# GpSimd's scatters of the last four groups, in rows or one and two at a time

## The chip, the core and the metric

The kernel runs on one core of one Trainium2 chip. Its time is device microseconds of one execution of the whole program. The core has five engines with a queue each: TensorE (PE in the profile; its weight loads are PEld), VectorE (DVE), ScalarE (ACT), GpSimd (POOL) and SyncE (SP, which here only starts DMAs). A queue with a q behind its name, POOLq or SPq, is the sequencer of that engine. Semaphores order what the engines do, and an instruction that waits holds back everything behind it on its own engine. The DMAs that SP starts run as "hardware" queue q1, those that GpSimd starts as "software" queue q0.

## The reference

A linear attention with decay, of 4 batches, 8 heads, 768 steps and 48 channels, is followed by a mixture of experts in which each of the 3072 tokens goes to the one expert with the largest logit.

```python
# attention, per batch and head; state is 48 x 48
cur   = (u * k_t) outer v_t
y_t   = r_t @ (state + cur)
state = w * state + k_t outer v_t

# experts: x is y, 3072 rows of 384 (all heads); 8 experts of width 1024
logits = x @ w_gate + modality_bias[modality_id]
e      = argmax(logits);  gate = softmax(logits)[e]
out    = gate * (relu(x @ w1[e]) @ w2[e])
```

The rows of `x` therefore have to be gathered by expert before the two expert products, and the result has to go back to the row of its token.

## The kernel before

**Units and groups.** The attention is cut into 24 units (`NU`): 6 chunks of 128 steps times 4 batches, chunk by chunk. A unit gives 128 tokens of 384 features. The routing works on groups of units, `GROUPS = ((0, 4), (4, 8), (8, 12), (12, 16), (16, 19), (19, 22), (22, 24))`. I call them group 0 to group 6; the last four are units 12 to 15 (four units), 16 to 18 (three), 19 to 21 (three) and 22 to 23 (two).

**What becomes of a group.** `token` adds the two parts of a unit's output and squares it on ScalarE (L431); `high` (ScalarE, L454) and `low` (VectorE, L458) write it as two 16-bit halves into the group's `row` tile, of which there are three in turn; `flip` transposes it by a DMA of SP; `logits` is on TensorE; `choose`, `count` and `place` find the expert and, in `posi`, the row of each token in a DRAM table `rows` that is sorted by expert. `sign` writes the token's number into the row (GpSimd). Then `send` (L570) scatters one unit, 128 rows of 1544 bytes, into `rows` with an indirect DMA whose descriptors GpSimd makes. There are 24 such sends.

**When a send is issued.** All engines are in an order written out by hand (`manual_schedule`), so the order of the Python calls is the order in each queue. In the loop over units (L1090 on) the units up to 20 issue one or two sends apart from each other, with GpSimd's elementwise work (`decay` L311, `carry` L318, `own_keys` L323) between them. From unit 21 on (`late`) this is left out and the sends come in rows: group 3's four sends at the end of unit 21, group 4's three in the tail after the last unit's `token`, and group 5's three and group 6's two directly behind each other in the tail. With `spaced=True` each is preceded by a memset of one element (`gap`, L569).

**Experts that start early.** While the attention still runs, nine blocks of 128 rows of the first expert (`s_` functions, slots 0 to 8) are computed between the units: `s_turn` has SP transpose the rows from `rows` into one of two halves of `mxT` (L893), `s_up` is 36 matmuls with f16 weights in two parts (L906), `s_high` and `s_low` make the halves of the hidden layer (L910, L915), `s_down` is 24 matmuls (L980, L985), `s_take` scales on ScalarE, and `s_give` sends the result to the output with an indirect DMA of GpSimd (L876), which I call an output send.

**The tail.** After the loop (L1168 on) the last unit and slots 5 to 8 are interleaved with the routing of groups 4, 5 and 6. `setup3` writes constants on GpSimd, `ends` and `pads` have SP write nine blocks of empty rows behind the experts' rows (L803), `jobs` makes the table of the remaining blocks on VectorE. The first block after that, `turn(0, self.s_row(NE), m2, group="first")`, waits for all rows of the table that it may read; `up("a")` on it begins the steady loop over the remaining blocks (L1320 on), whose time the order of the sends does not touch.

**Who waits for a send.** The code declares the sends independent of each other ("rows") and of the `s_turn`s ("read", rows that were there before). It does not declare them independent of the first block after the slots ("first"). The `row` tile of group 6 is that of group 3, so the first write of group 6 (`token` of unit 22, ScalarE L431) waits until group 3's sends have read theirs.

Of the kernel before, what the change touches and what calls it, by code (L numbers as in the profile page):

```python
# [13 lines left out]
I16 = mybir.dt.int16  # L14
# [4 lines left out]
P = 128  # L19
B, H, S, D = 4, 8, 768, 48  # L20
# [3 lines left out]
DM = H * D  # L24
# [23 lines left out]
ROW, CODE, MORE = range(3)  # L48
SP, ACT, AD = (mybir.EngineType.SP,), (mybir.EngineType.Activation,), (mybir.EngineType.Activation, mybir.EngineType.DVE, mybir.EngineType.Pool)
WQ = 2 * WC // NQ  # L50

LOW, TOP = 64 - D, 64 + D
HALVES = slice(0, 64), slice(64, TOP)
# [2 lines left out]
class _Kernel:  # L56
# [121 lines left out]
    def setup2(self):  # L178

        nc, c = self.nc, self.c  # L180
        wg, bias, mod = self.raw_in
        self.gap = c.tile([1, 1], F32, name="gap")
        self.ctl = c.tile([1, 64], I32, name="ctl")
        wq = c.tile([P, DC * E], F32, name="wgsq")
        ssq = c.tile([P, 1], F32, name="wgssq")
        nc.scalar.activation(wq, wg, AF.Square, accum_out=ssq)
        yield
        self.tri = c.tile([P, P], F16, name="tri")
        nc.scalar.copy(self.tri, self.mask)
        yield  # L190
        pt = self.ps_r.tile([P, 512], F32, tag="r", name="pswg")
        nc.tensor.matmul(pt[:, :1], self.ones, ssq, start=True, stop=True)
        s = c.tile([P, 1], F32, name="wgs")
        self.wginv = c.tile([P, 1], F32, name="wginv")
        yield from self.pow2_(pt[:, :1], s, self.wginv, WGC, "wg")
        self.wghl = c.tile([P, DC, 2, E], F16, name="wghl")
        wg3 = wg.rearrange("p (d e) -> p d e", d=DC)
        nc.scalar.activation(self.wghl[:, :, 0, :], wg3, AF.Copy, scale=s)
        yield
        nc.vector.scalar_tensor_tensor(self.wghl[:, :, 1, :], wg3, s, self.wghl[:, :, 0, :], ALU.mult, ALU.subtract)  # L200
        yield
        NTT = NT // P
        mf = c.tile([P, NTT], F32, name="modf")
        nc.scalar.copy(mf, mod.rearrange("p (t w) -> p t w", w=2)[:, :, 0])
        yield
        mg = c.tile([P, NTT], F32, name="modg")
        nc.scalar.activation(mg, mf, AF.Copy, scale=-1.0, bias=1.0)
        yield
        self.lb = c.tile([P, NTT, E], F32, name="lb")
        lb2 = c.tile([P, NTT, E], F32, name="lb2")  # L210
        bc = lambda ap: ap.unsqueeze(1).to_broadcast([P, NTT, E])
        tb = lambda ap: ap.unsqueeze(2).to_broadcast([P, NTT, E])
        nc.vector.tensor_mul(self.lb, tb(mf), bc(bias[:, E:]))
        yield
        nc.vector.tensor_mul(lb2, tb(mg), bc(bias[:, :E]))
        yield
        nc.vector.tensor_add(self.lb, self.lb, lb2)
        yield
# [338 lines left out]
    def sign(self, u):  # L557
        n, lo = u["n"], u["lo"]
        row = u["row"][:, :n, 2 * DM + 2 :].bitcast(I32).rearrange("p b o -> p (b o)")
        self.nc.gpsimd.tensor_copy(row, self.tok[:, lo : lo + n])  # L560

    def send(self, u, k, spaced=False):

# [252 lines left out]
    def norm(self, junk, q):  # L816
        self.nc.scalar.activation(junk, self.raw[:, q * WQ : (q + 1) * WQ], AF.Square, accum_out=self.ssq[:, q : q + 1])

# [21 lines left out]
    def piece(self, q, part, parts, n=1):  # L840
        w = WQ // parts
        return slice(q * WQ + part * w, q * WQ + part * w + n * w), self.ws[:, 2 * q // NQ : 2 * q // NQ + 1]

# [149 lines left out]
    def run(self):  # L993
# [20 lines left out]
        self.slot = {}  # L1014
        junk = m.tile([P, WQ], F16, name="junk", bufs=1)
        groups = {}
# [15 lines left out]
        def chain(*gs):  # L1032
            for g in gs:
                yield from g
# [37 lines left out]
        def route(i, d, f, *args):  # L1072
            for lo, hi in GROUPS:
                if hi - 1 + d == i and lo in groups:
                    f(groups[lo], *args)

        def each(i, *fs):
            for f in fs:
                if live(i):
                    f(i)  # L1080
# [9 lines left out]
        for i in range(NU - 1):  # L1090
            each(i + 5, self.turned)
            each(i + 4, self.lines)
            each(i + 1, self.scores, self.own_keys)
            route(i, 3, lambda u: fills.append(self.choose(u)))
            route(i, 5, lambda u: fills.append(chain(self.place(u), self.ahead(ahead[u["lo"]], u)) if u["lo"] in ahead else self.place(u)))
            up, down = ups.get(i), ups.get(i - 1)
            if up is not None:
                self.s_up(up, 0)
            if down is not None:
                self.s_high(down, 1)  # L1100
                self.s_down(down, 0)
            self.token(i - 1) if i else None
            if ups.get(i - 2) is not None:
                self.s_take(ups[i - 2])
            if i and i - 1 == self.grp["lo"]:
                groups[i - 1] = self.grp
            fill()
            each(i, self.taken) if i else None
            for j in range(2):
                each(i - 1, lambda i: self.state(i, j))  # L1110
                fill()
            if down is not None:
                self.s_low(down, 1)
                self.s_due(down)
            begin.get(i, lambda: None)()
            late = i >= NU - 3
            for k in range(2):
                if not late:
                    for d in (6, 7):
                        route(i, d, self.send, 1)  # L1120
                if k == 0:
                    each(i + 3, self.decay)
            if ups.get(i - 2) is not None:
                self.s_give(ups[i - 2])
            each(i + 2, self.carry)
            route(i, 4, self.sign)
            each(i + 2, self.keys)
            if i:
                fac = self.factor(i - 1)
                for _ in fac:  # L1130
                    fill()
            self.own(i, 0)
            each(i - 1, self.high)
            for j in range(2):
                each(i + 1, lambda i: self.causal(i, j))
                fill()
            self.own(i, 1)
            each(i - 1, self.low)
            if up is not None:
                self.s_high(up, 0)  # L1140
                self.s_low(up, 0)
            fill()
            each(i - 1, self.flip)
            fill()
            self.values(i)
            if up is not None:
                self.s_up(up, 1)
            if down is not None:
                self.s_down(down, 1)
            for p in range(2):  # L1150
                for h in range(2):
                    c, r = divmod(i + 1 - 2 * p - h, B)
                    if r == 0 and 0 < c < NCH - 1:
                        self.fade(c, slice(2 * p, 2 * p + 2), range(2 * h, 2 * h + 2))
            if any(hi - 1 + d == i for lo, hi in GROUPS for d in (4, 5)):
                fill(99)
            route(i, 2, self.logits)
            route(i, 4, self.count)
            if late:
                for d in (5, 6, 7):  # L1160
                    route(i, d, self.send, B, True)
            for f in at.get(i, ()):
                f()
            for k in turns.get(i, ()):
                self.s_turn(k)


        g4, g5 = (groups.get(lo) for lo, _ in GROUPS[-3:-1])  # L1168
        run = lambda g, n: [next(g, None) for _ in range(n)]
        i, j = NU - 2, NU - 1  # L1170
# [5 lines left out]
        self.own(j, 1)  # L1176
        p4 = chain(self.place(g4), self.ahead(ahead[g4["lo"]], g4))
        run(p4, 99)
        self.s_take(4)
        fac = self.factor(i)  # L1180
        run(fac, 9)
# [5 lines left out]
        self.values(j)  # L1187
        self.s_up(5, 1)
        self.token(j)
        self.send(g4, B, True)  # L1190
        self.s_give(4)
        g6 = groups.setdefault(GROUPS[-1][0], self.grp)
        self.setup3()
# [5 lines left out]
        run(fac, 9)  # L1199
        self.s_high(5, 1)  # L1200
        self.high(j)
        self.s_low(5, 1)
        self.low(j)
        self.logits(g5)
# [19 lines left out]
        self.s_low(6, 1)  # L1224
        run(c6, 9)
        run(p5, 99)
        self.send(g5, B, True)
        self.s_down(6, 0)
        self.count(g6)
        self.s_down(6, 1)  # L1230
        run(p6, 99)
        self.send(g6, B, True)
        self.s_take(6)
        self.s_up(7, 0)
        self.s_high(7, 0)
# [56 lines left out]
        def second_half(code):  # L1292
            with tc.If(code % 8 > 3) as first:
# [6 lines left out]
                nc.gpsimd.tensor_tensor(self.whi[:, hi], self.raw[:, hi], sc.to_broadcast([P, 512]), ALU.mult)  # L1300
                mid = slice(sl.start - WQ, hi.start)
                nc.scalar.activation(self.whi[:, mid], self.raw[:, mid], AF.Copy, scale=sc)
# [75 lines left out]
```

## Time and profile before

| | |
|---|---|
| median of 3 runs | 377.9 us (375.51 to 379.3) |
| profiled execution | 379.97 us |
| its span, first to last instruction | 378.0 us |
| busy: PE, DVE, ACT, POOL | 345.8, 226.0, 178.3, 164.1 us |
| mean granted TensorE clock | 0.952 of full |
| sends to `rows` | 24, mean 1001 ns on GpSimd |
| `rk` products on GpSimd | 24, mean 1274 ns |

A line of the timeline gives start and duration in us, the engine, the line of the kernel, the operation, the tiles (written <- read), the shape, how many instructions were merged, and in brackets how long the engine had been idle before and what ended that. "issue" means that the engine waited for nothing that the profile shows. A line of the view by windows gives, for a stretch, the busy time of each engine with its count of instructions in brackets, then the granted TensorE clock, the busy share of the DMA engines, and GB/s. The view of waits gives total, number and longest wait in us.

### The profile page before, as it was taken

The numbers are of one execution on the slowest core, as the hardware profiler recorded it, in microseconds if no ns is written. First come the engines' busy times: TensorE is split into PE (matmuls) and PEld (weight loads), VectorE is DVE, ScalarE is ACT, GpSimd is POOL, SyncE is SP. The second block draws the span as 40 slices with busy tenths as digits, with TensorE's granted clock in tenths as the row PEclk, the third lists the DMA queues.
The fourth block names the chain that finished last, engine by engine and source line by source line (L and its number), as shares of the span: only waits on it lengthen the run. The fifth ranks groups of instructions, "written<-read, shape, count | busy, mean of one in ns | idle before, by whom it ended". The sixth has DMA issues, their size and how long they took to land. (4 is left out here: it accounts for less than half of the span.)

```text
span 378.0 us, 14983 instructions
## 1 busy us (share of the span) xinstructions
PE 345.8 (91%) x5387; PEld 271.7 (72%) x5387; DVE 226.0 (60%) x762; ACT 178.3 (47%) x479; POOL 164.1 (43%) x231
## 2 busy tenths in 40 slices
PE   8799999697999999969899699998999999999883
PEld 3577777566978878758787477886677778877661
DVE  7668999889897875844447342338633323224861
ACT  7467875696756756554431112228022222256811
POOL 7996867736637855170424311123421111202631
PEclk9999999959699999987989899999999999999998
DMA  6999999999938998560333532111862122111110
GB/s 170 267 178 185 225 199 249 301 243 211 224 58 223 240 280 188 84 197 4 109 61 107 209 87 64 42 42 42 316 91 57 42 46 59 42 42 42 42 54 4
DMA packets 60749, 50.29 MB, mean 133 GB/s; under 512 B 46872, under 2 KB 54311, under 8 KB 60448
## 3 DMA queue, kind: packets, MB, share of 16 engines
q1 hardware_dynamic: 57504, 40.21, 48.1%
q0 software_dynamic: 3200, 9.47, 7.2%
q8 instruction: 30, 0.49, 0.5%
q14 instruction: 15, 0.12, 0.1%
HBM read 28.39 MB, written 11.83 MB: 106 GB/s over the span
## 5 line engine op out<-in xcount | busy, mean ns | idle before, releaser
L906 PEld LDWEIGHTS <-whi 128*128 128x128 f16 x1248 | 76.5, 101 | 8.7 <-issue 5.7
L980 PEld LDWEIGHTS <-hh 128*128 128x128 f16 x416 | 38.2, 98 | 31.2 <-ACT hh L910 6.3
L906 PE MATMUL phb<-mxT,whi 128*128 128x128 f16 x768 | 50.9, 219 | 0.0
L352 ACT ACTIVATE dv<-kv,d 128x48 f32<-128x48 f32 x192 | 47.9, 323 | 3.5 <-DVE d L344 3.3
L323 POOL TENSOR_TENSOR rk<-rc,kc 128x512 f32<-128x512 f32 x24 | 30.6, 1274 | 39.9 <-DVE posi L552 13.8
L906 PEld LDWEIGHTS <-wlo 128*128 128x128 f16 x624 | 39.8, 101 | 3.2 <-DVE wlo L852 3.2
L910 ACT ACTIVATE hh<-phb 128x256 f16<-128x256 f32 (+1 forms) x48 | 21.4, 454 | 42.3 <-PE po L980 18.0
L915 DVE SCALAR_TENSOR_TENSOR hl<-phb,hh 128x256 f16<-128x256 f32 (+1 forms) x48 | 24.2, 511 | 24.8 <-ACT hh L910 14.5
L906 PE MATMUL phs<-mxT,whi 128*128 128x128 f16 x432 | 32.7, 237 | 3.8 <-issue 3.8
L311 POOL TENSOR_TENSOR rc<-ud,powr 128x512 f32<-128x512 f32 (+1 forms) x27 | 32.8, 1219 | 3.2 <-PE py L394 1.5
L401 PE MATMUL py<-kv,at 128*64 128x48 f32 x768 | 30.0, 229 | 4.6 <-issue 4.6
L570 POOL DMA_INDIRECT rows<-row,posi x24 | 24.0, 1001 | 22.8 <-issue 17.1
L372 DVE TENSOR_TENSOR at<-psc,mask 128x512 f32<-128x512 f32 x48 | 31.6, 682 | 3.6 <-PE psc L366 3.3
L906 PE MATMUL phb<-mxT,wlo 128*128 128x128 f16 x384 | 30.0, 219 | 2.5 <-DVE wlo L852 2.5
L401 PEld LDWEIGHTS py<-kv,at 128*64 128x64 f32 x768 | 27.7, 146 | 6.0 <-issue 5.7
L990 DVE TENSOR_SCALAR fac<-mt,wf 128x1 f32<-128x1 f32 x17 | 3.6, 212 | 44.7 <-ACT otb L866 39.0
L985 PEld LDWEIGHTS <-hl 128*128 128x128 f16 x208 | 19.2, 97 | 14.8 <-issue 3.3
L980 PE MATMUL po<-wlo,hh 128*128 128x384 f16 x136 | 28.0, 326 | 1.7 <-DVE wlo L852 1.7
L980 PE MATMUL po<-whi,hh 128*128 128x384 f16 x136 | 28.6, 327 | 0.9 <-ACT hh L910 0.9
L866 ACT ACTIVATE otb<-po,fac 128x384 f32<-128x384 f32 x16 | 9.2, 578 | 42.1 <-PE phb L906 37.1
L366 PE MATMUL psc<-rc,kc 48*64 48x128 f32 (+1 forms) x768 | 28.3, 286 | 0.8 <-issue 0.8
L366 PEld LDWEIGHTS psc<-rc,kc 48*64 48x64 f32 (+1 forms) x768 | 22.1, 139 | 9.1 <-issue 4.1
(251 smaller groups left out, 641.7 us busy)
## 6 DMA issues: line engine op xcount, KB each, us to landing
ud<-in_pd SPq DMA_DIRECT2D x24, 384.0 KB
kv<-in_pt SPq DMA_DIRECT2D x24, 384.0 KB
raw<-in_w SPq DMA_DIRECT2D x12, 512.0 KB
raw<-in_w SPq DMA_DIRECT2D x2, 1536.0 KB, 6.4
rows<-pad SPq DMA_DIRECT2D x10, 193.0 KB
rows<-row,posi POOLq DMA_INDIRECT x24
xT<-row SPq DMA_TRANSPOSE x23
xn<-rows SPq DMA_TRANSPOSE x17
```

The source lines that it names most:

```text
L311: nc.gpsimd.tensor_mul(u["rc"][:, s], u["rT"][:, s], self.powr[:, s])
L323: nc.gpsimd.tensor_mul(u["rk"], u["rc"], u["kc"])
L352: nc.scalar.activation(u["dv"][:, sl], u["v"][:, sl], AF.Copy, scale=u["d"][:, h : h + 1])
L366: nc.tensor.matmul(u["ps"][j][s, pr * P : (pr + 1) * P], u["kc"][r, pr, s], u["rc"][r, pr, :], start=True, stop=True)
L372: nc.vector.tensor_mul(u["at"][:, j * NPR : (j + 1) * NPR, :], u["ps"][j].rearrange("p (q t) -> p q t", q=NPR), self.mask.unsqueeze(1).to_ ...
L401: nc.tensor.matmul(py[t, sl], u["at"][:, j * NPR + pr, t], u["v"][:, sl], start=c == h == 0, stop=h == H - 1, skip_group_check=True)
L570: i = nc.gpsimd.indirect_dma_start(out=self.rows, out_offset=bass.IndirectOffsetOnAxis(ap=u["posi"][:, b : b + 1], axis=0), in_=u["row"][: ...
L906: self.nc.tensor.matmul(ph[:, q * P : (q + 1) * P], w[:, c0 : c0 + P], self.xT[:, xq, t * P : (t + 1) * P], start=i == q == 0, stop=i == l ...
L910: self.nc.scalar.activation(self.hh[:, f0 : f0 + fb, t * P : (t + 1) * P], p3, AF.Relu)
L915: self.nc.vector.scalar_tensor_tensor(self.hl[:, f0 : f0 + fb, r], p3, 0.0, self.hh[:, f0 : f0 + fb, r], ALU.max, ALU.subtract)
L980: self.nc.tensor.matmul(po[:, :DM], self.hh[:, f, t * P : (t + 1) * P], w[:, c0 : c0 + DM], start=n == q == f == 0, stop=False)
L985: self.nc.tensor.matmul(po[:, :DM], self.hl[:, f, t * P : (t + 1) * P], self.whi[:, c0 : c0 + DM], start=False, stop=f == FB - 1)
```

## The change

The rows of sends are taken apart. In units 21 and 22 group 3's four sends are issued two to a unit: one where the earlier units have them, and one after the second half of `own` on ScalarE. What holds the latter back is the new function `rest`, which on GpSimd copies one element of a tile that another engine has just written into `gap`, so that GpSimd waits for that engine, or, without an argument, clears a tile of 128 x 1536 16-bit numbers (`pause`). In the tail group 4's sends are issued one by one: after `place`, after the last unit's square, and after the last unit's `high`. Group 5 sends two, then there is a `pause`, then its third and group 6's first, another `pause`, and group 6's second. The number of sends and what each writes stay as they are.

```diff
+PAUSE = 1536
...
+        self.pause = c.tile([P, PAUSE], I16, name="pause")
...
+    def rest(self, of=None):
+
+        v = self.nc.gpsimd
+        if of is None:
+            v.memset(self.pause, 0)
+        else:
+            v.tensor_copy(self.gap, of)
...
             late = i >= NU - 3
-            for k in range(2):
-                if not late:
-                    for d in (6, 7):
-                        route(i, d, self.send, 1)
+            for k in range(1 if late else 2):
+                for d in (6, 7):
+                    route(i, d, self.send, 1)
                 if k == 0:
                     each(i + 3, self.decay)
...
             self.own(i, 1)
+            if late:
+                for d in (6, 7):
+                    route(i, d, lambda u: (self.rest(self.ctx_[i]["dv"][:1, DM - 1 :]), self.send(u, 1)))
             each(i - 1, self.low)
...
             route(i, 4, self.count)
-            if late:
-                for d in (5, 6, 7):
-                    route(i, d, self.send, B, True)
...
         run(p4, 99)
+        self.send(g4, 1, True)
         self.s_take(4)
...
         self.token(j)
-        self.send(g4, B, True)
+        self.rest(self.grp["ssq"][:1, self.ctx_[j]["at_g"] :][:, :1])
+        self.send(g4, 1)
         self.s_give(4)
...
         self.high(j)
+        self.rest(self.ctx_[j]["x16"][:1, :1])
+        self.send(g4, 1)
         self.s_low(5, 1)
...
         run(p5, 99)
-        self.send(g5, B, True)
+        self.send(g5, 2, True)
         self.s_down(6, 0)
         self.count(g6)
         self.s_down(6, 1)
         run(p6, 99)
-        self.send(g6, B, True)
+        self.rest()
+        self.send(g5, 1)
+        self.send(g6, 1, True)
+        self.rest()
+        self.send(g6, 1)
         self.s_take(6)
```

## The prediction

> **What bounds the kernel now.** I began with the page.
>
> ```profile
> span 378.0 us, 14983 instructions
> PE 345.8 (91%) x5387; PEld 271.7 (72%) x5387; DVE 226.0 (60%) x762; ACT 178.3 (47%) x479; POOL 164.1 (43%) x231
> ```
>
> TensorE is busy for 91% of the span and GpSimd for 43%. The chain that ended last covers only the last few microseconds, so I went on to TensorE's waits, over the span.
>
> ```profile
> PE py L401 <- issue: 4.6, 8, 1.1
> ...
> PE phs L906 <- issue: 3.8, 7, 1.2
> ...
> PE psc L366 <- issue: 0.8, 1, 0.8
> ...
> PE pst L339 <- issue: 0.7, 2, 0.5
> PE pst L408 <- issue: 0.5, 2, 0.3
> ```
>
> These are waits for nothing that the profile shows: 8.4 us in the first two rows, 2.0 us in the others. The timelines of TensorE and GpSimd place the 8.4 us: all of it beside the three rows of sends. The view by windows round the rows:
>
> ```profile
> 163.00:170.00 7.00, 3.58 (x60) 2.99 (x59) 1.80 (x6) 2.42 (x7) 5.85 (x12) 0.81 0.64 185
> ...
> 184.00:189.00 5.00, 3.62 (x62) 3.04 (x60) 2.24 (x10) 1.07 (x2) 3.91 (x8) 0.88 0.36 128
> ...
> 207.00:213.00 6.00, 2.48 (x24) 1.51 (x22) 0.22 (x1) 0.45 (x1) 3.76 (x8) 0.89 0.64 234
> ```
>
> The first count in brackets is TensorE's matmuls, and the third number from the right its granted clock. While GpSimd sends, TensorE gets through few matmuls and its clock is cut. No other engine is full there: VectorE and ScalarE wait for TensorE. So these stretches bound the time, and a row is paid twice, as standstill and as a slow clock.
>
> **What a row costs.** I time TensorE's steps in the disturbed units against the same steps undisturbed.
>
> ```profile
> 157.08 1.09 PE L401 MATMUL py<-kv,at 128*64 128x48 f32 x32
> 158.00 0.60 PE L339 MATMUL pst<-uw,rk 112*64 112x2 f32 x16
> ...
> 161.40 1.51 PE L906 MATMUL phs<-mxT,whi 128*128 128x128 f16 x24
> ...
> 163.51 0.88 PE L394 MATMUL py<-st,rc 112*64 112x96 f32 x16
> 164.23 0.50 PE L401 MATMUL py<-kv,at 128*64 128x48 f32 x10
> ...
> 170.94 2.74 PE L906 MATMUL phs<-mxT,whi 128*128 128x128 f16 x24
> ...
> 174.58 1.10 PE L366 MATMUL psc<-rc,kc 64*64 64x128 f32 x32
> ...
> 184.78 0.74 PE L401 MATMUL py<-kv,at 128*64 128x48 f32 x20
> ...
> 191.52 0.60 PE L481 MATMUL pr<-wghl,xT 128*128 128x16 f16 x18
> ...
> 207.17 0.33 PE L906 MATMUL phs<-mxT,whi 128*128 128x128 f16 x3
> ...
> 215.00 1.46 PE L980 MATMUL pos<-whi,hh 128*128 128x384 f16 x6
> ```
>
> Undisturbed, 32 matmuls of L401 take 158.00 - 157.08 = 0.92 us, the L339 behind them 0.60, and one `s_up` (36 of L906) 163.51 - 161.40 = 2.11.
> - First row, unit 21: L401 starts at 164.23, so `s_up` should at 164.23 + 0.92 + 0.60 = 165.75; it starts at 170.94, 5.19 late, and then takes 174.58 - 170.94 = 3.64, which is 1.53 over 2.11. Together 6.7 us.
> - Second row, last unit: L401 at 184.78, `s_up` due from 185.70 to 187.81; it is through at 191.52. 3.7 us.
> - Third row: `s_up` of slot 7 from 207.17, due at 209.28, through at 215.00. 5.7 us.
>
> Sum 16.1 us for 12 sends, 1.34 us each. This is the most that there is to win.
>
> **What the changed kernel keeps of it.** The same trace has sends that do not stand in a row, and one new step has a near relative in it:
>
> ```profile
> 123.43 1.02 POOL L570 DMA_INDIRECT rows<-row,posi  x1
> ...
> 125.92 1.02 POOL L570 DMA_INDIRECT rows<-row,posi  x1 [0.16 <-issue]
> ```
> ```profile
> 44.03 0.75 POOL L244 MEMSET pad<- 128x772 int16 x1
> ...
> 162.25 1.02 POOL L876 DMA_INDIRECT out<-ots,puts  x1 [0.56 <-issue]
> ...
> 163.57 0.97 POOL L570 DMA_INDIRECT rows<-row,posi  x1 [0.21 <-DVE er L510]
> ...
> 167.38 0.96 POOL L570 DMA_INDIRECT rows<-row,posi  x1 [0.22 <-DVE hl L915]
> ...
> 183.76 1.01 POOL L570 DMA_INDIRECT rows<-row,posi  x1 [14.00 <-issue]
> ...
> 203.72 0.97 POOL L570 DMA_INDIRECT rows<-row,posi  x1 [4.72 <-DVE base L554]
> ...
> 208.83 0.97 POOL L570 DMA_INDIRECT rows<-row,posi  x1 [0.22 <-issue]
> ```
>
> The first 12 sends stand 2.5 us apart or more (123.43 and 125.92), and all issue waits outside the rows make 2.0 us: 0.17 a send, and at worst the longest single one, 0.8. In a row four sends start within 167.38 - 163.57 = 3.81 us, one every 1.27.
>
> Group 3 (four sends): one in unit 21 ahead of the output send of 162.25, one after `own`, two in unit 22. Group 4 (three): one at about 183.8 as before, two at the last unit's square and `high`, microseconds apart. Seven alone, of which one comes about 2 us behind an output send: 7 x 0.17 = 1.2 us (bounds 0 and 7 x 0.8 = 5.6).
>
> Groups 5 and 6 (five): pair, pause, pair, pause, one. A pause clears 1536 numbers; 772 take 0.75, so about 1.5 us. The five start at 203.7, 205.0, 207.7, 209.0 and 211.7 by the old clock. That is between the two cases: inside a pair 1.3 us, across a pause 2.7. Between 0.17 and 5.7 / 5 = 1.14 us a send I take the middle, 0.65: 3.3 us (bounds 0.9 and 5.7).
>
> Kept: 1.2 + 3.3 = 4.5. Won: 16.1 - 4.5 = 11.6 us (bounds 16.1 - 0.9 = 15.2 and 16.1 - 11.3 = 4.8).
>
> **What the moved and added steps hold up.** Nothing is taken out but eight `gap` memsets, and GpSimd is idle for more than half of the span. The new waits:
>
> ```profile
> 177.02 1.00 ACT L352 ACTIVATE dv<-kv,d 128x48 f32<-128x48 f32 x4
> ...
> 181.72 0.47 ACT L431 ACTIVATE row<-py 128x384 f16<-128x384 f32 x1
> ```
> ```profile
> 227.81 1.50 PE L906 MATMUL pha<-mxT,whi 128*128 128x128 f16 x24
> ```
> ```profile
> 224.00:225.00 1.00, 0.90 (x7) 0.53 (x7) 0.89 (x4) 0.09 (x1) 0.00 (x0) 1.00 0.01 0
> ```
> ```profile
> out<-otb,putb POOLq DMA_INDIRECT x16, 2.6
> ```
>
> - The copy behind `own` in unit 21 waits for ScalarE. Behind it on GpSimd stands unit 23's `rk`, which so far stood behind the whole row; it comes earlier.
> - Group 3's last send now waits for `own` of unit 22 (over at 178.02). Unit 22's square at 181.72 overwrites that buffer. Copy and issue about 0.5, then 2.6 as an output send takes to land: 3.1 of the 3.7 us between them. Both move ahead with TensorE. Cover 0.6 us; should landing take a microsecond longer, ScalarE is late by 0.4, and TensorE has slots 5 and 6 to do meanwhile. Cost 0 to 1, I take 0.
> - Group 4's two copies hold up the output send of slot 4 and `setup3`, which nobody needs before the job table.
> - The two pauses put the last send from 208.83 to 211.7, 2.9 us, and hold up slot 6's output send as much. The first block after the slots must wait for the last send, landed at about 211.7 + 2.6 = 214.3. Its DMA is over by 224.0 (DMA share 0.01 from there), after SP's empty rows, and TensorE turns to it at 227.81. So 3.8 us of TensorE's gain in the third row are free of SP; I count on 5.7 - 3.3 = 2.4.
>
> Span 378.0 - 11.6 = 366.4; profiled execution 379.97 - 11.6 = 368.4. The median, 377.9, is 2.1 under that execution: 377.9 - 11.6 = **366.3 us**.
>
> **A rule and the rows.** Of the clock: in 184 to 189 it was 0.88 on average, although TensorE was busy for 3.62 of 5 us. The Trainium skill (TensorE: Matmul & The Clock Gate, Part 1) says that the clock falls back to half after at least one idle window of about 3.4 us. By that page short gaps such as the changed kernel may keep cost no clock, and the kept 4.5 would be some 1 us less by my estimate; by the row, shorter gaps close together do cost it. I go by the row, as 0.65 a send contains a share of it.
>
> **The rivals.**
> - *The sends are not what stops TensorE.* The profile names no releaser; the sends are only beside it. Then nothing comes back: 377.9. Against it: no issue wait of over 0.8 us anywhere else. A sentence on it from the Trainium skill (SBUF — State Buffer, SBUF: two separate sides): engine ports and DMA ports are disjoint and cannot contend, so by that page the sends' traffic does not slow matmuls through SBUF; the low counts beside the rows are then of another cause, or of another path. 0.07. That the standstill belongs to profiled executions alone comes out the same; but the profiled one is only 2.1 us over the median, not 16.
> - *The price goes with the send, not with the row*: 12 x 1.34 stay. 377.9. Against it the 0.17 a send of the first twelve. 0.05.
> - *Something else is late*: group 3's buffer, or SP's blocks, take back 2 to 4 us: 369.5. For it the cover of 0.6 us above. 0.10.
> - *Slower: the cold clock spreads.* Each of the seven lone sends stops TensorE for the longest single wait, 0.8, and each time the next step runs cold, 1.53 as behind the first row: 2.33 x 7 = 16.3. The last row lasts 2.9 longer beside SP's empty rows: 5.7 + 2.9 = 8.6. Together 24.9 in place of 16.1: 386.7. It turns slower once a lone send costs over (16.1 - 8.6) / 7 = 1.07. Against it that the rows' windows alone lose clock beside sends so far. 0.08.
>
> **How the numbers follow.** 0.70 is left for the forecast, with its own range of 377.9 - 15.2 = 362.7 to 377.9 - 4.8 = 373.1. With the rival at 369.5 that holds 0.80. The runs of before spread by 2.4 below and 1.4 above their median, so I put the range at 361 to 375. One per cent, 3.8 us, is about what a measurement of this kernel can tell from no change. Faster by more: 0.70 + 0.10 = 0.80, all of both, as even 4.8 us is over it; the same 0.07 + 0.05 = 0.12; slower 0.08.
>
> **What would show it.** In the changed profile TensorE's issue waits at L401 and L906 of the tail fall from 8.4 to 2 or 3 us; the clock in units 21 to 23 stays near full; the `s_up` of unit 22 and that of the last unit take 2.1 us; what is left stands at 205 to 215 less the gain, beside the last five sends. The steady loop is as long as before and only starts earlier. I am wrong if the waits stay as long with sends apart, if ScalarE's square L431 waits for a DMA, or if TensorE at L906 `pha` waits for the transposed rows.

## The result, and the profile after

| | before | after |
|---|---|---|
| median of 6 runs each | 378.91 us (375.51 to 381.69) | 365.17 us (363.18 to 367.28) |
| ratio, 95% interval | | 0.967 (0.9631 to 0.9709) |
| profiled execution, its span | 379.97, 378.0 us | 365.14, 363.3 us |
| mean granted TensorE clock | 0.952 | 0.968 |

The changed kernel is 13.7 us faster by the medians; the forecast was 366.3, that is 11.6 us. A ratio here and below leaves out the executions that took over 1.5% longer than the fastest of the same kernel (three of the ten of `p_last`, for instance), so it can differ from the quotient of the medians. In the changed kernel the lines of the code stand lower: `send` is L580, `s_up` L916, `own` L403, `s_down` L990 and L995, `s_high` L920, the square L433, and `rest` is L568 and L570.

First the page of the changed kernel, then TensorE's waits over its span. A row of the waits gives total, number and longest in us.

```profile
span 363.3 us, 14983 instructions
PE 337.2 (93%) x5387; PEld 265.1 (73%) x5387; DVE 230.3 (63%) x762; ACT 178.2 (49%) x479; POOL 167.2 (46%) x229
```
```profile
PE pos L990 <- ACT hh L920: 2.1, 2, 1.2
```

The two rows that carried 8.4 us before, the issue waits at `own` and at `s_up`, are gone altogether. The other issue waits are 1.3 us (0.7 at L368 and 0.6 at L341; 2.0 before). New is a wait of 2.1 us of the slots' `s_down` for ScalarE's `hh`. The view by windows has the same stretches as before. Two lone sends, one and none now start in them, and the clock is full in all three:

```profile
163.00:170.00 7.00, 7.00 (x145) 6.07 (x143) 5.19 (x16) 4.21 (x13) 3.65 (x5) 1.00 0.51 128
184.00:189.00 5.00, 5.00 (x80) 4.35 (x79) 1.53 (x9) 1.98 (x4) 3.72 (x18) 1.00 0.49 140
207.00:213.00 6.00, 5.90 (x59) 3.82 (x57) 2.98 (x14) 1.18 (x2) 0.89 (x2) 1.00 0.39 107
```

GpSimd's sends of groups 3 to 6 in the changed kernel's timeline (start, duration); group 3's first, at 156.41, stands ahead of these lines:

```profile
163.80 0.98 POOL L580 DMA_INDIRECT rows<-row,posi  x1 [0.16 <-issue]
166.24 1.02 POOL L580 DMA_INDIRECT rows<-row,posi  x1 [0.17 <-issue]
171.87 0.98 POOL L580 DMA_INDIRECT rows<-row,posi  x1 [0.52 <-issue]
...
195.20 0.97 POOL L580 DMA_INDIRECT rows<-row,posi  x1 [0.22 <-issue]
196.18 1.40 POOL L568 MEMSET pause<- 128x1536 int16 x1
...
201.57 0.98 POOL L580 DMA_INDIRECT rows<-row,posi  x1 [0.17 <-issue]
```

And TensorE's steps in the same stretch:

```profile
163.84 1.09 PE L403 MATMUL py<-kv,at 128*64 128x48 f32 x32
...
165.49 1.51 PE L916 MATMUL phs<-mxT,whi 128*128 128x128 f16 x24
...
167.60 1.10 PE L368 MATMUL psc<-rc,kc 64*64 64x128 f32 x32
...
180.96 0.60 PE L483 MATMUL pr<-wghl,xT 128*128 128x16 f16 x18
...
192.01 0.50 PE L990 MATMUL pos<-whi,hh 128*128 128x384 f16 x2 [0.81 <-ACT hh L920]
...
195.37 1.50 PE L916 MATMUL phs<-mxT,whi 128*128 128x128 f16 x24
...
199.39 0.81 PE L990 MATMUL pos<-whi,hh 128*128 128x384 f16 x4
201.45 0.50 PE L990 MATMUL pos<-whi,hh 128*128 128x384 f16 x2 [1.25 <-ACT hh L920]
...
213.31 1.50 PE L916 MATMUL pha<-mxT,whi 128*128 128x128 f16 x24
```

The same steps of both kernels, from the starts of these rows and of those of before (there 164.23, 174.58, 191.52, 205.16 and 227.81). The fourth start of before is that of slot 7's first half:

```profile
205.16 1.50 PE L906 MATMUL phs<-mxT,whi 128*128 128x128 f16 x24
```

| from, to | before | after | won |
|---|---|---|---|
| `own` of unit 21 to the next scores (first row) | 10.35 | 3.76 | 6.6 |
| scores to the gate's logits, `pr` (second row) | 16.94 | 13.36 | 3.6 |
| logits to `s_up` of slot 7 | 13.64 | 14.41 | -0.8 |
| `s_up` of slot 7 to the first block, `pha` (third row) | 22.65 | 17.94 | 4.7 |

Together 14.1 us; unit 21 began 0.4 earlier, so `pha` starts 227.81 - 213.31 = 14.5 us earlier, and the spans differ by 14.7. All of the gain lies at the three rows, none of it in the steady loop.

### The profile page after: what moved, and what is told of

It reads as the page before. It is cut to its first block, busy times and chain, and to the rows that moved or that the text cites. A ratio compares the mean times of both kernels' runs of the same rounds, so it can differ in the third digit from the quotient of the medians.

```text
span 363.3 us, 14983 instructions
## 1 busy us (share of the span) xinstructions
PE 337.2 (93%) x5387; PEld 265.1 (73%) x5387; DVE 230.3 (63%) x762; ACT 178.2 (49%) x479; POOL 167.2 (46%) x229
## 5 line engine op out<-in xcount | busy, mean ns | idle before, releaser
L916 PEld LDWEIGHTS <-whi 128*128 128x128 f16 x1248 | 73.6, 99 | 3.7 <-issue 0.9
L990 PEld LDWEIGHTS <-hh 128*128 128x128 f16 x416 | 38.0, 98 | 32.9 <-ACT hh L920 8.0
L916 PE MATMUL phb<-mxT,whi 128*128 128x128 f16 x768 | 50.8, 219 | 0.0
L920 ACT ACTIVATE hh<-phb 128x256 f16<-128x256 f32 (+1 forms) x48 | 21.3, 454 | 42.0 <-PE L990 13.7
L916 PEld LDWEIGHTS <-wlo 128*128 128x128 f16 x624 | 38.2, 99 | 3.2 <-DVE wlo L862 3.2
L925 DVE SCALAR_TENSOR_TENSOR hl<-phb,hh 128x256 f16<-128x256 f32 (+1 forms) x48 | 24.2, 511 | 24.7 <-ACT hh L920 14.5
L313 POOL TENSOR_TENSOR rc<-ud,powr 128x512 f32<-128x512 f32 (+1 forms) x27 | 31.8, 1184 | 2.7 <-PE py L396 1.5
L916 PE MATMUL phb<-mxT,wlo 128*128 128x128 f16 x384 | 30.0, 219 | 2.6 <-DVE wlo L862 2.6
L995 PEld LDWEIGHTS <-hl 128*128 128x128 f16 x208 | 19.3, 97 | 14.7 <-issue 3.1
L990 PE MATMUL po<-wlo,hh 128*128 128x384 f16 x136 | 28.0, 326 | 1.7 <-DVE wlo L862 1.7
L580 POOL DMA_INDIRECT rows<-row,posi x24 | 24.1, 1006 | 11.6 <-DVE base L556 3.6
L990 PE MATMUL po<-whi,hh 128*128 128x384 f16 x136 | 28.3, 327 | 1.0 <-ACT hh L920 1.0
L885 POOL TENSOR_TENSOR seenb<-otb,putb 128x1 int32<-128x1 int32 x16 | 5.0, 310 | 52.8 <-ACT otb L876 50.0
L368 PEld LDWEIGHTS psc<-rc,kc 64*64 64x64 f32 (+1 forms) x768 | 21.5, 136 | 9.8 <-issue 4.8
L916 PE MATMUL phs<-mxT,whi 128*128 128x128 f16 x432 | 28.5, 224 | 0.0
L368 PE MATMUL psc<-rc,kc 64*64 64x128 f32 (+1 forms) x768 | 27.6, 280 | 0.9 <-issue 0.7
L403 PE MATMUL py<-kv,at 128*64 128x48 f32 x768 | 28.0, 229 | 0.0
```

The costliest lines, as they stand in the source:

```text
L313: nc.gpsimd.tensor_mul(u["rc"][:, s], u["rT"][:, s], self.powr[:, s])
L368: nc.tensor.matmul(u["ps"][j][s, pr * P : (pr + 1) * P], u["kc"][r, pr, s], u["rc"][r, pr, :], start=True, stop=True)
L403: nc.tensor.matmul(py[t, sl], u["at"][:, j * NPR + pr, t], u["v"][:, sl], start=c == h == 0, stop=h == H - 1, skip_group_check=True)
L580: i = nc.gpsimd.indirect_dma_start(out=self.rows, out_offset=bass.IndirectOffsetOnAxis(ap=u["posi"][:, b : b + 1], axis=0), in_=u["row"][: ...
L916: self.nc.tensor.matmul(ph[:, q * P : (q + 1) * P], w[:, c0 : c0 + P], self.xT[:, xq, t * P : (t + 1) * P], start=i == q == 0, stop=i == l ...
L920: self.nc.scalar.activation(self.hh[:, f0 : f0 + fb, t * P : (t + 1) * P], p3, AF.Relu)
```

## The experiments

The theory: sends 1.27 us behind each other stop TensorE and then cost it clock, and sends further apart do not. The rivals: something else that the reordering moved brought the gain; or it is plain traffic, the number of descriptors or GpSimd's busy time that counts, and not sends close together. Each group of runs was made on one chip together with the kernel before: it took 378.74 us there (`p_` kernels and `d_row`), 359.67 (`d_narrow`, `d_spaced`, `d_sp`, `b_waits`), 378.22 (`c_` kernels and `d_mix`) and 377.96 (`a_row`). The second of these chips is a story of its own, told below. The ratio of a run is to the kernel before on the same chip, with its 95% interval. The four `d_` kernels and `d_mix` write tables that nobody reads; all else is computed as before.

**p_units: the kernel before with the part of units 21 and 22 alone.** The three `p_` kernels also have `rest` and the tile `pause` of the change.

```diff
-            for k in range(2):
-                if not late:
-                    for d in (6, 7):
-                        route(i, d, self.send, 1)
+            for k in range(1 if late else 2):
+                for d in (6, 7):
+                    route(i, d, self.send, 1)
...
+                    route(i, d, lambda u: (self.rest(self.ctx_[i]["dv"][:1, DM - 1 :]), self.send(u, 1)))
...
-                    route(i, d, self.send, B, True)
```

> The kernel before, with the change in units 21 and 22 alone: group 3's four sends two to a unit, groups 4, 5 and 6 as before. Theory (a row of sends on GpSimd stops TensorE and leaves its clock cold, each row by itself): the first row's 6.6 to 6.7 us come back, so about 372 us where before has 378.9, ratio 0.982; the issue waits at the values matmuls of unit 21 vanish, those of the second and third row stay. Rival (one row is enough to use up the gain, or the tail takes back what the units win): less than 3 us.

373.35 us, ratio 0.9845 (0.977 to 0.9921). In its profiled execution `s_up` of unit 21 follows `own` directly; two of the three clusters of issue waits are left:

```profile
PE phs L916 <- issue: 4.0, 6, 1.2
...
PE py L403 <- issue: 1.7, 4, 0.6
```

The first cluster is gone and the others stayed. The scores of unit 22 start at 167.95 in place of 174.58, 6.6 us earlier, and `pha` at 222.41 in place of 227.81, 5.4 earlier: the second row's stage took 17.72 in place of 16.94 and gave 0.8 back, the next 0.3.

**p_g4: the part of group 4 alone.**

```diff
         run(p4, 99)
+        self.send(g4, 1, True)
...
-        self.send(g4, B, True)
+        self.rest(self.grp["ssq"][:1, self.ctx_[j]["at_g"] :][:, :1])
+        self.send(g4, 1)
...
         self.high(j)
+        self.rest(self.ctx_[j]["x16"][:1, :1])
+        self.send(g4, 1)
```

> The kernel before, with the change for group 4 alone: its three sends one by one in the tail. Theory: the second row's 3.6 to 3.7 us come back, ratio 0.990. Rival (the tail is held by the transposed rows or by the routing, not by TensorE): under 1 us.

377.0 us, ratio 0.9958 (0.9922 to 0.9993): 1.6 us, less than expected. The issue waits of `own` in the last unit are gone. In the second row's stage (174.44 to 187.68) the kernel wins 16.94 - 13.24 = 3.7, as forecast. Then it loses 0.8 (187.68 to 202.12 is 14.44, in place of 13.64), as the changed kernel does, with a wait for ScalarE of 0.82. And its row of five comes at another point and costs 1.1 more: `s_up` of slot 7 to `pha` takes 225.86 - 202.12 = 23.74 in place of 22.65. So the price of a row isn't the same wherever it falls, and a part's own gain can be passed on to the next row.

**p_last: the part of groups 5 and 6 alone.**

```diff
-        self.send(g5, B, True)
+        self.send(g5, 2, True)
...
-        self.send(g6, B, True)
+        self.rest()
+        self.send(g5, 1)
+        self.send(g6, 1, True)
+        self.rest()
+        self.send(g6, 1)
```

> The kernel before, with the change for groups 5 and 6 alone: pair, pause, pair, pause, one. Theory: the third row's time comes back but for what the trace of the changed kernel still shows there, 4.3 to 4.7 us, ratio 0.988; the three parts then add up to the whole. Rival (pairs 1.3 us apart still stop TensorE, and the gain there came from the other two): 2 us or less.

Ratio 0.9847 (0.9802 to 0.9892), 5.8 us; the median of all ten executions is 374.04, 4.7 us under the kernel before. No line of its profile is shown, since the profiled execution took 379.19 us, as long as the kernel before. The three parts add to 1.55 + 0.42 + 1.53 = 3.5%, and the whole change is 3.3%: they add up within their intervals.

**a_row: the changed kernel with groups 5 and 6 back in one row.**

```diff
-        self.send(g5, 2, True)
+        self.send(g5, B, True)
...
-        self.rest()
-        self.send(g5, 1)
-        self.send(g6, 1, True)
-        self.rest()
-        self.send(g6, 1)
+        self.send(g6, B, True)
```

> The changed kernel with groups 5 and 6 sent in one row of five again, as before, groups 3 and 4 left apart. Theory (each row by itself stops TensorE, where the chip is one on which before takes about 378 us): 4 to 5 us over the changed kernel's 364.5 to 365.2, so 369 to 370, with 3 to 5 us of issue waits in slot 7, as the reverse of the run with the last part alone. Where before takes about 360 us: within 1 us of before and no issue waits beside the row. Rival (the parts do not add up): under 2 us, since the transposed rows or the job table end the tail there once the other rows are gone.

369.49 us, ratio 0.9769 (0.9729 to 0.981), 4.3 over the changed kernel's 365.17. This pair is the cleanest: up to `s_up` of slot 7 (195.38 here, 195.37 there) the two run alike. The five sends start at 193.93, 195.21, 196.49, 197.76 and 199.03. TensorE in the timeline of `a_row`:

```profile
197.39 0.50 PE L916 MATMUL phs<-mxT,whi 128*128 128x128 f16 x6
198.18 0.22 PE L916 MATMUL phs<-mxT,whi 128*128 128x128 f16 x1 [0.29 <-issue]
199.57 0.27 PE L916 MATMUL phs<-mxT,whi 128*128 128x128 f16 x2 [1.18 <-issue]
200.99 0.27 PE L916 MATMUL phs<-mxT,whi 128*128 128x128 f16 x2 [1.14 <-issue]
201.72 0.28 PE L916 MATMUL phs<-mxT,whi 128*128 128x128 f16 x2 [0.46 <-issue]
202.43 0.78 PE L916 MATMUL phs<-mxT,whi 128*128 128x128 f16 x11 [0.43 <-issue]
...
204.25 2.13 PE L990 MATMUL pos<-whi,hh 128*128 128x384 f16 x6
...
217.86 1.50 PE L916 MATMUL pha<-mxT,whi 128*128 128x128 f16 x24
```

A few matmuls pass, then TensorE stands for 0.3 to 1.2 us, five times: 3.5 us. What follows is at half clock (granted 0.50 from 204 to 206): six of `s_down` take 2.13, against 1.41 in the next slot of the same trace. `pha` is 217.86 - 213.31 = 4.55 later than in the changed kernel, about the 4.3 of the medians. The standstill begins at 197.89, 4.0 us after the first send has started, and goes on for 2.4 us after the last has left GpSimd (200.0). Here it lags GpSimd's issuing by about the time that an output send takes to land, 2.6 us in the profile of before. That would fit the transfers rather than GpSimd's own work, but it isn't shown: in the second row of before TensorE first stops 1.8 us after the first send has started and runs again 0.7 us after the last has left.

The stops do not answer the sends one by one. TensorE starts again 1.39, 1.42, 0.73 and 0.71 us after the start before, in the third row of before 1.46, 0.72, 0.73, 0.72 and 0.74: multiples of about 0.72, where the sends are 1.27 apart. What sets this step was not tested.

**d_row: the changed kernel and, at the end of unit 20, four more full sends directly behind each other.** This adds the suspected cost where nothing else was changed. The first column of `tok` holds 0 to 127, so each of these sends writes 128 rows in order and scatters nothing.

```diff
+    def extra(self, width, spaced=False):
+        for q in range(4):
+            to = self.dram.tile([P, width], I16, name=f"extra{q}")
+            if spaced and q:
+                self.rest()
+            self.nc.gpsimd.indirect_dma_start(
+                out=to,
+                out_offset=bass.IndirectOffsetOnAxis(ap=self.tok[:, 0:1], axis=0),
+                in_=self.pad[:, :width],
+                in_offset=None,
+            )
...
+            if i == 20:
+                self.extra(RW)
```

> The changed kernel with four more sends directly behind each other at the end of unit 20, of 128 rows of 1544 bytes from a tile of zeros into four DRAM tiles that nobody reads. GpSimd has nothing to do there for 5 us. Theory (the sends themselves stop TensorE): 4 to 7 us over the changed kernel, with issue waits beside the four and a cold clock behind them. Rival (TensorE stood for something else in the stages where the rows were): 0 to 1 us over it.

370.75 us, ratio 0.9818 (0.9757 to 0.9879): 5.6 us over the changed kernel's 365.17 of the first comparison, whose kernel before took 378.91 (378.74 here). The sends start from 150.74 to 154.60. TensorE in its timeline:

```profile
152.97 0.24 PE L534 MATMUL pr<-oh,warm 128*128 128x8 f16 x4
...
156.71 1.13 PE L368 MATMUL psc<-rc,kc 64*64 64x128 f32 x31 [0.94 <-issue]
```

The steps up to the scores' end take from 152.97 to 157.77; in the changed kernel, where the same start at 151.63 and end at 153.01, they take 1.4. So the row costs 3.4 us here. Of the 5.1 by which the profiled spans differ (368.4 and 363.3), 1.3 is there already at 152.97. The cold clock that was expected behind the row did not come: the scores take 1.13 us and the next six of `s_down` 1.15, as elsewhere.

**d_mix: three disturbances in one kernel.** Four sends of 32 bytes a row at the end of unit 14 (as many descriptors as four full ones, a 48th of the bytes), four plain DMAs of 128 rows of 1544 bytes by SP at the end of unit 18, and four full sends at the end of unit 20.

```diff
+    def extra(self, key, width, spaced=False):
+        for q in range(4):
+            to = self.dram.tile([P, width], I16, name=f"extra{key}{q}")
...
+    def plain(self):
+        for q in range(4):
+            to = self.dram.tile([P, RW], I16, name=f"plain{q}")
+            self.nc.sync.dma_start(to, self.pad)
...
+            if i == 14:
+                self.extra("n", 16)
+            if i == 18:
+                self.plain()
+            if i == 20:
+                self.extra("w", RW)
```

> The changed kernel with three additions that write to DRAM tiles nobody reads: four sends of 32-byte rows directly behind each other at the end of unit 14, four plain DMAs of SP of 197 KB each at the end of unit 18, four full sends directly behind each other at the end of unit 20. Each is read from the trace by itself. Theory: where before takes about 378, the full row costs 3 to 5 us of TensorE's time with issue waits, the narrow row and SP's DMAs under 1 us each (it needs both GpSimd's queue and full rows). Where before takes about 360, none of the three costs over 1 us. Rival (descriptors alone): the narrow row costs as much as the full one. Rival (writing to DRAM alone): SP's DMAs cost as much as the full row.

371.34 us, ratio 0.9812 (0.9761 to 0.9863), 6.8 over the changed kernel on the same chip (`c_after`, 364.5). Each disturbance has its place in TensorE's timeline; narrow sends, SP's DMAs (that row is SP's) and full sends in this order:

```profile
107.28 0.91 PE L403 MATMUL py<-kv,at 128*64 128x48 f32 x25
108.34 0.32 PE L403 MATMUL py<-kv,at 128*64 128x48 f32 x3 [0.16 <-issue]
...
109.83 0.20 PE L403 MATMUL py<-kv,at 128*64 128x48 f32 x1 [0.46 <-issue]
109.87 0.59 PE L410 MATMUL pst<-kv,kt 128*64 128x48 f32 x15
```
```profile
143.55 2.04 SPq L587 DMA_DIRECT2D plain<-pad  x4
```
```profile
143.32 1.48 PE L1012 MATMUL pos<-whi,hl 128*128 128x384 f16 x8
...
145.77 1.51 PE L933 MATMUL phs<-mxT,whi 128*128 128x128 f16 x24
...
152.52 0.22 PE L534 MATMUL pr<-oh,warm 128*128 128x8 f16 x3
...
156.17 1.13 PE L368 MATMUL psc<-rc,kc 64*64 64x128 f32 x31 [0.94 <-issue]
157.23 1.96 PE L1007 MATMUL pos<-whi,hh 128*128 128x384 f16 x6
...
161.61 0.63 PE L396 MATMUL py<-st,rc 112*64 112x96 f32 x10
```

- Narrow: `own` to the next step takes 109.87 - 107.28 = 2.59 in place of 0.92, 1.7 more. Under 1 us was expected.
- SP's plain DMAs: no issue wait, every step as long as elsewhere.
- Full: 161.61 - 152.52 = 9.09. The changed kernel takes 155.72 - 151.63 = 4.09 for the same steps, so it is 5.0 more, of which the half clock is a part: 1.96 for six matmuls that take 1.15 there.

1.7 + 5.0 = 6.7, and the kernel lost 6.8. That these agree so closely is partly luck: in the profiled executions TensorE is 1.05 us behind `c_after` already before the narrow sends (106.56 for 105.51), 2.75 behind after them (115.44 for 112.69), and only 1.56 when the full row begins (152.52 for 150.96). The same bytes written by SP's queue cost nothing, and as many descriptors with hardly any bytes cost a third. So neither the bytes alone nor the number of descriptors alone makes the price. The three stand in different units, beside different steps of TensorE, so that share is rough.

**c_before and c_after: the two kernels once more, beside `d_mix`,** both without an edit.

> The kernel before, unchanged, for a trace of it beside the next two. In the first set of runs it took 378.7 us, in the second 359.7, although it is the same program. Theory (how dear a row is differs from chip to chip): where it takes about 360, its three rows show no issue waits at the values matmuls and in slots 5 and 7; where it takes about 378, some 8 us of them. Rival (the 19 us are elsewhere, in the steady loop or in the loads): the rows stop TensorE for as long as in the first trace, and the loop or the start is shorter.

> The changed kernel, unchanged, timed against the kernel before on this chip. Theory: its gain is what the rows cost on the chip that it runs on; 13 to 14 us where before takes about 378, and 0 to 1 us, either way, where before takes about 360. Rival (the gain does not depend on the chip): 0.967 of before everywhere.

379.6 us in one run, and 364.5 us, ratio 0.9638 (0.9594 to 0.9682), 13.7 us as in the first comparison. The waits of `c_before`:

```profile
PE py L401 <- issue: 4.7, 8, 1.4
PE phs L906 <- issue: 4.1, 6, 1.2
```

8.8 us: the rows' standstill comes back in another execution. It isn't a matter of where the tiles lie either, since `p_units` has the new tile `pause`, which nothing uses there, and its second and third rows stop TensorE all the same.

**d_narrow, d_spaced, d_sp, b_waits: on the chip where the kernel before takes 359.67 us.** Each is the changed kernel with one edit, in this order: four narrow sends at the end of unit 20; four full ones there with a clearing of `pause` between them; four plain DMAs of SP there; and the two clearings between the last five sends replaced by waits for `hh` and `hl` of slot 7, with the sends moved behind these.

```diff
+            if i == 20:
+                self.extra(16)
```
```diff
+            if i == 20:
+                self.extra(RW, True)
```
```diff
+    def extra(self):
+        for q in range(4):
+            to = self.dram.tile([P, RW], I16, name=f"extra{q}")
+            self.nc.sync.dma_start(to, self.pad)
...
+            if i == 20:
+                self.extra()
```
```diff
-        self.rest()
-        self.send(g5, 1)
-        self.send(g6, 1, True)
-        self.rest()
-        self.send(g6, 1)
         self.s_take(6)
         self.s_up(7, 0)
         self.s_high(7, 0)
+        self.rest(self.hh[:1, 0, :1])
+        self.send(g5, 1)
+        self.send(g6, 1, True)
...
         self.s_low(7, 0)
+        self.rest(self.hl[:1, 0, :1])
+        self.send(g6, 1)
```

> The changed kernel with four more sends directly behind each other at the end of unit 20, as many rows (128 each) but of 32 bytes instead of 1544, into DRAM tiles that nobody reads. Theory A (the price is in the descriptors that GpSimd makes, one set per row whatever its length): as much as with full rows, 4 to 7 us over the changed kernel. Theory B (the price is in the bytes that are written): 0 to 1 us over it.

> The changed kernel with the four full sends at the end of unit 20, a clearing of 128 x 1536 16-bit numbers (1.4 us) between each two, so that they start 2.7 us apart and not 1.1. Theory (the price is the row's): 0 to 2 us over the changed kernel. Rival (the price goes with the send): as much as the same four in a row. The next product of GpSimd comes about 4 us later than in the changed kernel, which has room for it.

> The changed kernel with the same four times 197 KB written to DRAM at the end of unit 20 by four plain DMAs of SP, not by GpSimd. Theory A (it is GpSimd's making of descriptors or its queue): 0 to 1 us over the changed kernel. Theory B (it is the writing of rows to DRAM by whatever queue): as much as the four sends of GpSimd.

> The changed kernel without the two clearings: group 5's third and group 6's first send wait for the first half of slot 7's hidden layer (ScalarE), group 6's second for its low half (VectorE). No computation is changed. In the trace of the changed kernel VectorE's small instructions beside the clearings take 1.5 to 1.9 us in place of 0.16, and TensorE waits 1.25 us for ScalarE in slot 7. Theory (the clearings hold VectorE, and VectorE is not in the way): 0 to 1 us faster than the changed kernel. Rival (the sends are then too close, the last two 1.2 us behind the one before): 1 to 3 us slower than it.

360.87 us, 1.0063 (1.0024 to 1.0102); 361.89, 1.0074 (1.003 to 1.0118); 360.23, 1.0003 (0.9966 to 1.004); 360.68, 1.0034 (0.9997 to 1.0071). The expected times cannot be held against these, since on this chip the kernel before itself, with its three rows, is as fast as kernels without a row; nothing had led me to expect that. What the added steps cost can still be read against each other: over `d_sp`, 0.6 us for four narrow sends and 1.7 for four spaced ones, and no issue wait stands beside either. The four narrow sends of `d_narrow` are 1.27 us apart as in `d_mix`, where they left three. `b_waits` has a new wait of TensorE, and its SP waits ahead of that block:

```profile
PE pha L916 <- DMA mxT<-rows: 1.1, 1, 1.1
```
```profile
SPq L903 <- DMA rows<-pad: 2.8, 1, 2.8
```

There the first block waits for its transposed rows, the sign that the prediction named. By the profile it isn't the last send that makes them late: SP's turn waits for SP's own empty rows (`rows<-pad`). Whether the changed kernel itself gains or loses on this chip wasn't tried, and no trace of the kernel before was taken there.

## Why the prediction was right

**The price of the rows** was forecast as 16.1 us from the trace of before, 6.7 + 3.7 + 5.7. The stages won 6.6 and 3.6 at the first two rows. The row of five, put back in `a_row`, costs 4.55 against the changed kernel, and with the 1.25 that this one still waits there 5.8. So the method holds: time the same steps undisturbed, and take the difference. But the price isn't a constant. A dummy row of four costs 3.4 in `d_row` and 5.0 in `d_mix`, and the row of three, 3.7 in the trace that the forecast used, costs 2.3 in `c_before`, where the same steps take from 186.25 to 191.61 in place of the undisturbed 3.03. The clock, below, makes most of the difference, so that the parts came out so near to the forecast is in some part luck.

**The rivals.** That the sends aren't the cause falls by `d_row` and `d_mix`: added sends bring the same waits to a place that had none. That the price goes with the send falls by the changed kernel: 12 sends, no issue wait at `own` or `s_up`. A cold clock that spreads didn't come, the clock rose from 0.952 to 0.968. Group 3's buffer was not late: ScalarE's square of unit 22 waits for VectorE,

```profile
175.68 0.49 ACT L433 ACTIVATE row<-py 128x384 f16<-128x384 f32 x1 [0.70 <-DVE pr L546]
```

and `pha` doesn't wait for rows. SP's turn for it starts here:

```profile
209.71 1.26 SPq L903 DMA_TRANSPOSE mxT<-rows  x1
```

Its issuing is over at 210.97. The transfer takes longer: the DMA share is 0.96 in 211 to 212 and 0.18 in 212 to 213, so the rows are there about 1 us ahead of `pha`. Of the 3.8 us of cover for the two pauses about so much is left; in `b_waits` it was used up. What SP's turn waits for last is in both the DMA of the empty rows (1.6 us here), not a send.

**The term that was mis-sized is what the changed kernel keeps, 4.5 us.** The seven lone sends, put at 1.2, cost about 0.5, and the last five, put at 3.3 as issue waits, cost 1.25. Both come in another form: TensorE doesn't stop, but waits for ScalarE's `hh`, which starts late. ScalarE's timeline, one row of the kernel before and two of the changed kernel:

```profile
198.42 0.60 ACT L910 ACTIVATE hh<-phs 128x512 f16<-128x512 f32 x1 [1.43 <-PE phs L906]
```
```profile
188.53 0.60 ACT L920 ACTIVATE hh<-phs 128x512 f16<-128x512 f32 x1 [1.85 <-PE pr L483]
...
200.80 0.60 ACT L920 ACTIVATE hh<-phs 128x512 f16<-128x512 f32 x1 [2.62 <-PE phs L916]
```

In the kernel before slot 6's first `hh` starts 0.2 us after its matmuls are through (198.22, when TensorE's next step starts). In the changed kernel they are through at 187.90 and `hh` starts 0.63 later, between group 4's last send (187.17) and an output send (189.23). The routing on VectorE and the second `hh` come later by it, and TensorE waits 0.81 for that one in place of 0.28, which is 0.53. In slot 7 the matmuls of the second half are through at 199.39, and `hh` starts 1.2 us late, beside the second pair of sends: 1.25. `p_g4` has group 4's sends as here and a wait of 0.82, so this one doesn't come from the last sends. `d_sp` has the same sends and clearings on the chip of 359.67, and both `hh` start on time there (185.94 for 185.74, 196.97 for 196.71). So the order of the sends alone doesn't make `hh` late; by what path it is late wasn't tested. A smaller loss does come from TensorE being earlier: in slot 5 ScalarE's square of the last unit (181.18) now stands ahead of `hh` (181.65), and six of `s_down` take from 181.42 to 182.63, 1.21 in place of 0.98. Together 1.25 + 0.53 + 0.23 = 2.0 in place of 4.5: 16.1 - 2.0 = 14.1, which is the 14.1 of the stages.

**The clock.** The row was nearer than the rule. The Trainium skill (TensorE: Matmul & The Clock Gate, Part 1) has the clock fall after at least one idle window of about 3.4 us. In `d_mix` the matmuls behind the full row are at half speed (1.96 for 1.15), though the longest idle stretch was 0.94 us and matmuls ran between the stretches; in `a_row` the longest was 1.18. So idle stretches that follow closely can be enough. They aren't always: `d_row` has nearly the same stretches (0.60, 0.53, 0.55 and 0.94) and keeps the full clock behind them. The same window of `d_mix` and of `d_row`, the granted clock third from the right:

```profile
158.00:159.00 1.00, 1.00 (x5) 0.47 (x4) 1.00 (x4) 0.29 (x2) 0.00 (x0) 0.50 0.86 201
```
```profile
158.00:159.00 1.00, 1.00 (x8) 0.61 (x7) 0.94 (x4) 0.84 (x4) 0.00 (x0) 1.00 0.01 3
```

The second row of the kernel before differs likewise: behind it 23 matmuls take 2.61 us in one execution, and 22 take 1.39 in `c_before`. And a single stretch wasn't enough: behind the wait of 1.25 at 201.45 the changed kernel keeps its clock. So the choice to count the half clock into a row's price was right for the trace that was read, but another execution may not pay that part.

**What stays open** is by what path the sends stop TensorE. The Trainium skill (SBUF — State Buffer, SBUF: two separate sides) says that the ports of engines and of DMAs are disjoint and cannot contend. SP's plain DMAs, which read the same tile and write as many bytes for nothing, agree with it, so plain traffic isn't the path. Something about GpSimd's transfers is: their descriptors, or their signals at the end, for instance. These weren't told apart. Scattered writes aren't needed, since the dummy sends write their rows in order. Whether TensorE's own instructions reach it late beside the sends wasn't looked at either. And it isn't TensorE alone: in the kernel before, ScalarE's `hh` of slot 7 could have started at about 207.4, since its matmuls are through at 207.17, but its timeline has

```profile
212.56 0.60 ACT L910 ACTIVATE hh<-phs 128x512 f16<-128x512 f32 x1 [6.56 <-remote]
```

at the moment when TensorE gets going again. Whether ScalarE was stopped itself or got TensorE's signal late can't be seen; in the changed kernel its `hh` is late though TensorE has run on.

## What to carry to other kernels

When TensorE waits for nothing that the profile shows, put its timeline beside GpSimd's: a row of three to five indirect sends 1.27 us apart cost 2.3 to 6.7 us on most chips here, standstill and, in some executions, half clock together. Sends 2.4 us or more apart, and pairs, left no such stop. Price such a stall by timing the same steps undisturbed, and look next at the engines that TensorE waits for: ScalarE, late beside a lone send and a pair, kept back 0.5 and 1.25 us here. Measure on more than one chip before a gain of this kind is counted on, since on one of them the kernel before was already as fast as kernels without a row.

## What was not expected of the hardware

- **The price of rows seems to depend on the chip.** Where the other chips took 378 us for the kernel before, one took 359.67 (31 runs, 356.77 to 365.82), and there the ratio of `d_sp`, which has no row, is 1.0003. The kernels without rows are faster there too: the profiled execution of `d_sp` has a span of 357.5 us, that of the changed kernel in the first comparison 363.3. I infer from this, and from the narrow sends and ScalarE's `hh` that are undisturbed there, that rows cost little on it, but it isn't shown, as no full row of sends was profiled on that chip. What differs between the chips isn't known.
- **GpSimd's clearing holds VectorE.** In VectorE's timeline of the changed kernel a copy of 128x8 numbers beside the first clearing (196.18 to 197.58), and an operation as small beside the second (200.00 to 201.41):

```profile
196.04 1.57 DVE L697 COPY two<-idxf 128x8 f32<-128x8 f32 x1
...
199.56 1.88 DVE L712 TENSOR_SCALAR first_row<-en 128x8 f32<-128x8 f32 x1
```

The first took 0.16 us in the kernel before, the second 0.17. Both end when the clearing does. The Trainium skill (SBUF — State Buffer, SBUF: two separate sides) says that VectorE and GpSimd have a pair of ports in common, which one holds for its whole instruction while the other is blocked; these two rows agree. In the changed kernel no wait of TensorE for VectorE stands there, but in `d_sp`, with the same clearings, TensorE waits 0.5 us for VectorE's `hl` in slot 7, and in `b_waits`, without them, it doesn't. So a clearing as a pause isn't free.
